# A tuned attention kernel of 1415 operations, reordered by a second search: new order and engine tables, refitted durations

## The chip, the cores and the metric

One core of one Trainium2 chip. The metric is the device time of one execution in microseconds (us). A time is the median of several executions. The profile is that of one of them, and its span (first to last instruction) is about 1.7 us shorter than the time of the same execution.

## The reference, cut to what matters

Two attention blocks run on the same 2048 x 640 input with 32 heads of 20, and a sigmoid gate mixes them. Block A is linear attention with a softmax feature map: projections, exponentials of both signs, normalisation, a key-value matrix per head, then a query side. Block B walks over four segments of 512 tokens: causal softmax attention inside each, plus a memory of the earlier ones.

```python
for s in range(N):                                   # block B, N = 4 segments of 512 tokens
    logits = jnp.einsum('bhqd,bhkd->bhqk', qs, ks) * scale + mask
    a_dot = jnp.einsum('bhqk,bhkd->bhqd', _softmax(logits, axis=-1), vs)
    num = jnp.einsum('bhld,bhde->bhle', pq, M)        # M, z: memory of the segments before
    den = jnp.einsum('bhld,bhd->bhl', pq, z)[..., None] + 1e-06
    outs.append(g * num / den + (1.0 - g) * a_dot)
    M = M + jnp.einsum('bhld,bhle->bhde', phi(ks), vs)
...
kv = jnp.einsum('bhsf,bhsd->bhfd', phi_k, v)         # block A, over all tokens
num = jnp.einsum('bhqf,bhfd->bhqd', phi_q, kv)
...
return g * a + (1 - g) * b
```

## The kernel before

The program is a list of 1415 operations. Each has the engines on which it may run, a duration that the author gave it, and the tiles that it reads and writes. A planner in the program, run when the kernel is built, plays the five instruction streams forward in time. At each step it takes, among the operations that can start within 0.12 us of the earliest one, that of the lowest priority number `pr`. What it decides is the order on each engine, the side of the 113 copies out of PSUM that may go to ACT or DVE, and the place of each tile in PSUM and SBUF. No duration reaches the chip; the order, the side and the places do.

```python
o.engs, o.dur, o.fn, o.pr, ... = engs, dur, fn, pr + NUDGE.get(len(self.ops), 0.0), name, dma, lat
...
while done < n:                                      # the planner, cut
    for e in STREAMS:
        ...
        if len(o.engs) > 1:
            b = {o.engs[0]: BIAS.get(o.idx, 0.0)}    # the engine table: ACT looks b us faster
            f = s + o.dur[e] - b.get(e, 0.0)
            if any(max(free[x], s) + o.dur[x] - b.get(x, 0.0) < f - 1e-6 for x in o.engs if x != e):
                continue
        ...
        lim = max(free[e], mn) + DELTA               # DELTA = 0.12 us
        ch = min(((o.pr, o.idx, s, o) for s, o in cands if s <= lim))
```

The operations that the argument touches, with PE = TensorE, DVE = VectorE, ACT = ScalarE, POOL = GpSimd:

```python
# block B: scores (QK, PE) -> exp (ACT) -> causal mask of the diagonal blocks (POOL, 128 of them) -> PV (PE)
mask(0, lambda: ex[:, :, 0:128], [[0, 4], [1, 128]], 512, [(0, 0), (0, 1)])
# -> combine (DVE): cmb, cmbp read PSUM, cmba adds two SBUF tiles into oB
# block B memory: keys transposed by DMA, then phi on DVE and ACT, SBUF alone
self.dma("sp", lambda c=c: pk[:, :, 128 * c:128 * (c + 1)], qk[:, c, 1, :], ..., transpose=True, dur=(1.3 if n else 1.7), lat=3.0, name="kT")
self.op("dve", 0.52, lambda e, tl=tl, tm=tm: e.tensor_tensor(pk[:, tl, :], pk[:, tl, :], tm[:, :], ALU.min), ..., name="pkmin")
# block A key side (DVE): sum, reciprocal, normalise, running sum "acc" of two SBUF tiles
# the small weight w_phi: its load is issued from POOL once the last key weights ("last") have landed
self.dma("pool", self.wphi[:, :, :], ..., pr=-39, lat=6.0, name="wphi", after=[last])
```

The softmax here doesn't subtract the row's maximum and nothing guards it: scores larger than these inputs give would overflow.

Of the kernel before, what the change touches and what calls it, by code (L numbers as in the profile page):

```python
# [7 lines left out]
ALU = mybir.AluOpType  # L8
AX = mybir.AxisListType

NUDGE = {6: 1.6, 7: 1.65, 8: -2.2, 9: -0.45, 11: -1.7, 19: -3.95, 22: 3, 23: 1.8, 24: -1.5, 35: -11.8, 36: -2.7, 37: 5.05, 40: 11.15, 62: 0.7, 63:
         2.15, 64: -1.4, 65: -7.8, 66: 0.95, 67: 6.15, 68: 17.2, 69: 9.2, 70: 3.6, 71: 13.15, 72: 4.2, 75: -8.85, 77: 1.3, 93: 4.7, 94: 16.3, 95:
         -0.65, 97: -1.6, 99: -7.9, 101: -10.25, 103: -15.25, 105: 1.1, 106: 9.7, 107: -3.35, 108: -1.55, 109: -0.15, 111: -1.75, 112: 3.45, 113:
         -2.1, 114: -8.75, 119: -5.35, 121: 2.9, 122: 3.2, 124: -0.8, 125: -0.7, 127: 6.1, 129: 3.1, 131: 5.9, 133: -6.55, 135: 5.9, 143: -3.6, 146:
         -1.7, 155: 7.9, 162: -9.4, 163: -4.5, 164: -3.3, 166: -12, 170: -3.35, 174: 1.85, 179: -5.05, 180: 6, 181: -6.5, 183: -6.3, 187: -3.45, 188:
         -4.45, 190: -8.2, 192: -2.65, 193: -11, 194: -6.6, 196: -10.35, 197: -2.45, 200: -0.65, 202: -10.9, 204: -3.1, 205: -2.9, 206: -7.45, 207:
         -4.25, 208: -8.5, 209: -3.3, 210: -14.45, 211: -7.8, 213: 4.2, 217: 0.75, 218: -3.2, 219: -10.25, 221: 4.05, 222: -12.25, 223: 42.5, 224:
         -9.75, 226: -1.55, 230: 0.7, 231: 6.1, 234: -5.6, 235: -1.3, 236: 5.7, 237: -6.8, 239: -1.75, 241: 6, 243: -0.95, 247: 2.05, 248: 4.6, 249:
         -4.9, 250: -13.95, 251: 1.2, 252: -9.8, 253: 3.7, 254: 5.35, 256: -5.533, 260: -5.8, 261: -2.8, 266: 1.75, 267: 3.85, 268: 3.05, 269: 1.071,
         270: 0.85, 271: -5.1, 273: -4.55, 277: 3, 282: 9.4, 283: 6.85, 284: -9.6, 285: 0.95, 286: -8.15, 287: 2.65, 288: 11.9, 289: -5.25, 290:  # L20
         -0.15, 291: 6.15, 292: 2.352, 293: -1.4, 294: 7.3, 295: 4.35, 296: -1.7, 297: 8.55, 298: -9, 299: -2.3, 300: -5.05, 301: -2.05, 302: 1.6,
         303: 1.5, 304: 1.85, 306: -1.25, 307: -4.35, 309: -3.65, 310: 7.4, 311: -1.45, 313: -1.7, 315: 1.4, 319: -2.75, 321: 0.85, 322: 3.45, 323:
         0.25, 324: -9.9, 325: 4.027, 328: 0.85, 332: 2.7, 333: 5.65, 335: 0.85, 336: 0.5, 337: -2.8, 338: -0.8, 339: 0.85, 341: 1.55, 344: -3.85,
         345: 6, 348: 3.1, 350: 1.35, 352: -1.1, 358: 4.35, 359: 8.25, 360: 4.05, 363: 2.35, 366: 0.75, 367: 2.55, 368: 8.3, 369: 0.4, 373: 3.9, 377:
         -5.8, 383: -0.75, 384: -0.55, 385: -2.35, 386: -0.4, 387: 2.85, 388: -2.35, 389: 3.95, 390: -14.3, 392: 2.6, 397: -7.05, 400: 1.55, 401:
         13.3, 402: 2.35, 403: -2.85, 404: 3.75, 405: -2.9, 407: -5.45, 411: 2.05, 412: 1.75, 413: 3, 415: -0.8, 416: 2.45, 417: -7, 418: -2.65, 419:
         -3.75, 420: -57.2, 421: 13.65, 422: 1.2, 426: 1.55, 430: 3.95, 434: 1.95, 435: 6, 437: -2.15, 438: -1.75, 439: -10.85, 441: -0.8, 445: -0.95,
         446: -2.6, 449: 0.35, 453: 3.75, 455: 10.95, 456: -1.45, 457: -4.15, 458: 7.35, 466: -13.2, 467: -0.9, 468: -2.9, 469: 0.4, 470: 6.4, 471:
         -1.942, 473: -5.4, 475: -1.75, 479: -0.35, 483: -2.15, 484: 0.45, 485: -12, 486: -19.7, 487: -8.75, 488: -8.05, 490: -3.1, 491: -13.85, 492:
         -10.1, 494: 2.6, 498: 3.258, 499: -1.2, 509: 4.15, 510: -5.5, 511: 9.8, 512: -3.25, 513: -2.6, 514: 8.8, 515: 0.55, 516: 12, 517: 7.6, 518:  # L30
         1.2, 519: -15.923, 521: 0.6, 522: 1.5, 523: -5.35, 524: -0.4, 525: 6.35, 530: -0.035, 531: 6.5, 532: 4.4, 533: -3.8, 534: 0.25, 535: -6.4,
         536: 4.9, 537: 3.15, 538: 2.672, 539: 14.3, 540: -2, 541: 3.35, 542: 2.85, 543: 6.7, 544: 0.007, 545: -3.65, 546: 0.5, 547: -9.45, 548:
         -1.95, 558: 1.65, 559: 4.45, 561: 4.1, 563: -4.15, 564: 0.1, 565: -1.95, 567: -0.25, 570: 1.8, 571: 0.2, 573: 3.5, 574: 21.8, 576: 4.25, 577:
         2.6, 578: 1.5, 579: -9.5, 581: 3.15, 582: 3.3, 583: 4.4, 584: 10.8, 586: 13.25, 587: 5.9, 590: 0.65, 591: 2.4, 592: -5.486, 594: 10, 596:
         -5.5, 597: -0.6, 600: 5.4, 604: -2.4, 605: -0.75, 608: 25.7, 610: -6.8, 611: -6.05, 612: -10.2, 616: -8.4, 619: 5.1, 620: 6.2, 626: -3.8,
         627: 3.05, 630: -28.25, 631: -13.3, 634: 4.85, 635: -8.65, 636: 5.15, 638: 2.55, 639: 0.85, 647: 11.35, 649: 1.85, 653: -2.35, 654: -1.35,
         658: 3.6, 659: 3.5, 660: -2.072, 662: -15.35, 664: -3.3, 668: -1.45, 672: 7.55, 673: 10.05, 678: 4.9, 679: -2.05, 683: -2.2, 687: -4.05, 688:
         2.05, 690: 10.05, 693: 4.75, 694: -3.2, 696: -3.55, 698: -3.55, 702: -2.45, 704: -2.45, 706: -1.65, 707: -6, 710: -8.75, 712: 14.75, 713:
         -2.8, 714: 10.25, 715: 3.15, 717: -3.7, 721: 1.45, 722: -5.1, 725: -8.9, 726: 0.25, 727: 6.4, 728: 5.1, 733: 0.35, 734: 2.7, 735: 18.4, 736:
         8.7, 737: 6.55, 738: 25.05, 739: 0.8, 740: 11.5, 741: 8.3, 742: 2.2, 743: 7.75, 744: 3.7, 745: -4.95, 746: 5.7, 747: -3, 748: 2.8, 753: 2.45,  # L40
         755: -0.35, 757: 5.35, 759: 0.574, 760: -6.65, 761: 0.3, 763: -0.233, 764: 2.35, 765: 6.2, 767: 3.5, 768: 5.5, 769: 5.75, 770: 2.8, 771:
         -1.45, 781: 2.2, 784: 0.45, 787: 16.15, 790: -7.7, 791: -0.85, 794: 1.6, 800: 14.35, 801: 7.1, 802: 4.15, 803: 21, 804: 12.15, 805: 6.2, 806:
         2.45, 807: 5.2, 809: 18.6, 810: 4.05, 811: 9.2, 812: 8.95, 813: 19.25, 814: 4.35, 816: 6.15, 817: 9.1, 819: -1.1, 823: -1.6, 827: -1.3, 828:
         -1.9, 834: -2.7, 835: -5.85, 838: -1.6, 842: 9.2, 843: -0.45, 845: 54.95, 849: 0.7, 850: -5.8, 853: -1.4, 857: -5.4, 860: 15.5, 861: 3.05,
         862: 2.2, 865: 6.6, 867: 26.85, 868: -6, 869: 3.15, 872: -12.3, 876: 3.95, 877: 11.35, 881: 10.1, 882: 3.85, 883: -1.35, 884: -3.55, 885:
         6.9, 887: 3.35, 891: -1.95, 895: -3.45, 896: -11.95, 900: 6.05, 902: -2.5, 903: 12.15, 904: -5.35, 906: -3.85, 910: -10.45, 911: -2.4, 917:
         0.05, 919: 7, 921: -13.35, 925: -12.75, 929: 7.15, 930: 6.35, 936: 1.45, 938: 1.25, 946: 4.95, 951: -2.5, 952: -9.6, 953: -7.2, 955: 4.85,
         959: -3.7, 961: -3.5, 962: -0.95, 963: 2.15, 967: -1.85, 968: 14.1, 969: 6.35, 970: -4.6, 971: 0.5, 972: -3.95, 973: 0.95, 975: -2.55, 976:
         14.9, 977: -5.4, 979: 9.25, 981: 0.1, 982: -4.7, 983: -4.75, 984: 0.85, 985: -7.75, 988: 4.1, 990: -1.75, 991: 1.45, 992: 0.45, 995: 1.8,
         997: 5.85, 999: 0.65, 1001: 9.85, 1003: -0.65, 1004: 4.7, 1005: 5.1, 1006: -6.1, 1007: 4.2, 1008: 0.85, 1009: 0.4, 1010: 5.15, 1011: 2.85,  # L50
         1012: 1.35, 1013: 1, 1014: -1.3, 1015: -1.15, 1016: 7.5, 1018: 10.8, 1019: 12.05, 1020: 0.25, 1021: -9.8, 1022: -3.95, 1023: 0.6, 1024: 5,
         1025: 5.85, 1026: -1.05, 1027: 3.6, 1029: -1.9, 1031: 0.3, 1034: 1.5, 1035: 1.45, 1036: -10.55, 1037: 3.55, 1038: 15.25, 1040: -0.65, 1041:
         5.25, 1042: -0.5, 1045: 0.1, 1047: -3.8, 1048: 8, 1051: 7.25, 1052: -4.4, 1053: -5.6, 1054: -3.05, 1055: 1.8, 1056: -0.4, 1058: -2.9, 1059:
         1.115, 1061: -0.15, 1062: 2.05, 1063: -1.7, 1064: -3.5, 1065: 5.3, 1066: -0.9, 1067: -7.6, 1068: 4.85, 1069: -2.2, 1070: -0.25, 1072: -6.9,
         1073: 1.9, 1075: -2.2, 1076: -5.7, 1077: -3.05, 1078: -3.05, 1079: 3.3, 1080: 2.464, 1081: 1.75, 1083: -1.1, 1084: 1.9, 1086: -1.1, 1087:
         -3.75, 1088: -8.6, 1090: 5.25, 1091: 2.85, 1092: 2.25, 1095: 1.95, 1097: -5.7, 1098: 1.95, 1101: 8.2, 1103: 0.4, 1104: 3.4, 1105: -7.75,
# [25 lines left out]
DH = 20  # L82
NT = 16
NCH = 5
# [90 lines left out]
class Graph:  # L175
# [6 lines left out]
    def op(self, engs, dur, fn, R=(), W=(), pr=0.0, claim=(), name="", dma=False, lat=0.0, after=()):  # L182
        o = Op()
        if isinstance(engs, str):
            engs = (engs,)
        if not isinstance(dur, dict):
            dur = {e: dur for e in engs}
# [356 lines left out]
class GatedMix(Graph):  # L544
# [399 lines left out]
    def b_mem(self, n):  # L944
# [5 lines left out]
        pk = self.sbt("pk", [128, 4, D], BF16, self.p_pk)  # L950
# [541 lines left out]
```

## Time and profile before

| | before |
|---|---|
| time, median of 4 (lowest, highest) | 321.23 us (321.08, 321.29) |
| span of the profile | 319.6 us |
| PE busy / idle | 297.3 / 22.3 us |
| DVE busy, 40 to 160 us | 115.6 of 120 us |
| granted clock | 1.0 throughout |

The lines for this are in the prediction. Two things to keep in mind: a matmul is drawn longer than it occupies PE, so idle time on PE is the better number; and lines are those of the program, so a helper's line stands for many operations.

### The profile page before, as it was taken

What the parts mean: (1) busy time and instruction counts of PE and PEld (TensorE: products, weight loads), DVE (VectorE), ACT (ScalarE), POOL (GpSimd) and SP (SyncE); (2) the same over time, 40 slices, a digit from 0 to 9 for tenths busy, and PEclk for the clock granted to TensorE, in tenths of its full rate; (3) what the DMA queues carried; (4) which work ended last, traced back from release to release, by engine and by line L of the source; (5) the groups of instructions that cost most, each with busy time, mean ns of one, the idle gap of its engine ahead of it and who ended that gap; (6) DMA issues with size and microseconds to landing.
All of it is one profiled execution on the core that took longest, in us unless ns stands there. A gap on an engine that the chain in (4) does not pass through costs nothing.

```text
span 319.6 us, 8900 instructions
## 1 busy us (share of the span) xinstructions
PE 297.3 (93%) x3822; PEld 174.5 (55%) x3822; DVE 245.9 (77%) x475; ACT 252.0 (79%) x302; POOL 110.5 (35%) x169
## 2 busy tenths in 40 slices
PE   8989899799899999879989999999999999988986
PEld 3444565366455565635565464756365565645664
DVE  5646898999999899999999996715775556857660
ACT  4377899988899889689988998769986869576612
POOL 6549223423243334235450234133222413223300
PEclk9999999999999999999999999999999999999999
DMA  7999884625314525972380102782044320521212
GB/s 246 294 217 195 101 145 80 138 43 92 76 21 84 106 43 83 112 132 49 116 175 1 24 2 22 128 128 55 23 43 64 84 62 11 55 60 27 64 23 82
DMA packets 70960, 28.01 MB, mean 88 GB/s; under 512 B 62410, under 2 KB 69002, under 8 KB 70922
## 3 DMA queue, kind: packets, MB, share of 16 engines
q1 hardware_dynamic: 70858, 27.41, 45.6%
q8 instruction: 30, 0.49, 0.7%
q0 software_dynamic: 64, 0.03, 0.1%
q14 instruction: 8, 0.07, 0.1%
HBM read 7.57 MB, written 4.59 MB: 38 GB/s over the span
## 4 chain that ended last, share of the span: by engine, by line
PE 54%; DVE 22%; ACT 15%; POOL 3%; DMA 2%; issue 2%; DVEq 0%; POOLq 0%
PE ps L1392 10%; PE ps L1104 8%; PE ps L896 6%; PE ps L1191 5%; PE ps L1293 5%; PE ps L1040 4%; ACT exb L1064 3%; ACT exb L1053 3%; DVE z L1206 3%; DVE E L1209 3%; ACT ET L1298 2%; DMA wphi<-in_A_w_phi_dram 2%; PE ps L1393 2%; ACT exb L1073 2%; PE ps L1354 2%; ACT E L1198 2%
## 5 line engine op out<-in xcount | busy, mean ns | idle before, releaser
L1058 POOL TENSOR_SCALAR_AFFINE_SELECT exb<-exb 128x512 bf16<-128x512 bf16 x96 | 69.9, 730 | 151.7 <-ACT exb L1053 81.4
L1053 ACT ACTIVATE exb<-ps 128x1024 bf16<-128x1024 f32 x64 | 62.1, 1024 | 11.1 <-PE ps L1040 11.0
L1064 ACT ACTIVATE exb<-ps 128x2048 bf16<-128x2048 f32 x32 | 60.0, 1876 | 7.7 <-PE ps L1040 7.6
L1104 PE MATMUL ps<-v1B,exb 128*128 128x42 bf16 (+1 forms) x1280 | 41.7, 181 | 3.0 <-DVE cb L1150 1.0
L1104 PEld LDWEIGHTS ps<-v1B,exb 128*128 128x128 bf16 x1280 | 38.8, 96 | 9.5 <-POOL exb L1058 2.8
L896 PE MATMUL ps<-xT,WB 128*128 128x512 bf16 x175 | 42.1, 380 | 1.4 <-DVE oB L1145 0.9
L1040 PE MATMUL ps<-qk 20*128 20x128 bf16 (+3 forms) x512 | 31.7, 301 | 4.2 <-ACT exb L1073 1.7
L1077 POOL TENSOR_SCALAR_AFFINE_SELECT exb<-exb 128x512 bf16<-128x512 bf16 x32 | 22.9, 736 | 30.5 <-ACT exb L1073 30.5
L1073 ACT ACTIVATE exb<-ps 128x2048 bf16<-128x2048 f32 x16 | 30.0, 1876 | 2.4 <-PE ps L1040 2.4
L896 PEld LDWEIGHTS ps<-xT,WB 128*128 128x128 bf16 x175 | 15.4, 98 | 21.0 <-issue 2.2
L1191 PE MATMUL ps<-WkA,xT 128*128 128x512 bf16 x80 | 23.5, 380 | 2.8 <-ACT exb L1053 1.1
L1198 ACT ACTIVATE E<-ps 128x640 bf16<-128x640 f32 x32 | 22.6, 705 | 4.3 <-PE ps L1192 3.8
L1209 DVE TENSOR_TENSOR E<-E,z 128x1280 bf16<-128x1280 bf16 x16 | 24.9, 1556 | 0.2
L917 PE MATMUL ps<-WvB,xT 128*128 128x512 bf16 x80 | 23.8, 380 | 1.1 <-DVE oA L1361 0.6
L1206 DVE TENSOR_REDUCE z<-E 128x64 f32<-128x1280 bf16 x16 | 23.6, 1474 | 1.6 <-ACT E L1198 1.5
L1298 ACT ACTIVATE ET<-ps 128x512 bf16<-128x512 f32 x40 | 22.9, 600 | 2.3 <-PE ps L1293 1.8
L1293 PE MATMUL ps<-xT,WqA 128*128 128x512 bf16 x100 | 24.1, 380 | 0.4 <-DVE ET L1337 0.4
L1191 PE MATMUL ps<-WvA,xT 128*128 128x512 bf16 x80 | 23.4, 380 | 0.5 <-ACT E L1198 0.4
L1392 PE MATMUL ps<-Wo,oTA 128*128 128x512 bf16 x75 | 22.0, 380 | 0.1
L1392 PE MATMUL ps<-Wo,oTB 128*128 128x512 bf16 x75 | 21.9, 379 | 0.0
L1040 PEld LDWEIGHTS ps<-qk 20*128 20x128 bf16 x512 | 8.9, 92 | 22.9 <-issue 6.7
L864 ACT ACTIVATE out<-ps 128x640 bf16<-128x640 f32 (+1 forms) x13 | 8.6, 663 | 14.9 <-PE ps L1393 13.3
(139 smaller groups left out, 598.7 us busy)
## 6 DMA issues: line engine op xcount, KB each, us to landing
out_dram<-out SPq DMA_DIRECT2D x15, 160.0 KB, 2.0
scr<-qk SPq DMA_DIRECT2D x16, 120.0 KB
qk<-scr SPq DMA_DIRECT2D x16, 120.0 KB
stq<-in_B_wq_dram SPq DMA_DIRECT2D x5, 160.0 KB, 4.2
WvB<-in_B_wv_dram SPq DMA_DIRECT2D x1, 800.0 KB, 5.3
WvA<-in_A_wqkv_dram SPq DMA_DIRECT2D x1, 800.0 KB, 7.8
Wo<-in_A_wo_dram SPq DMA_DIRECT2D x1, 800.0 KB
Wo<-in_B_wo_dram SPq DMA_DIRECT2D x1, 800.0 KB
```

The costliest lines, as they stand in the source:

```text
L896: r = e.matmul(self.pf(pt, 0, 0, LSEG), lhsT=self.WB[:, w, kc, 128 * c:128 * (c + 1)], rhs=xT[:, kc, LSEG * n:LSEG * (n + 1)], start=(kc = ...
L1040: r = e.matmul(self.pf(pts[i][0], pts[i][1], c0, N), lhsT=qk[32 * i:32 * i + DH, gg, 1, 128 * j:128 * (j + 1)], rhs=qk[32 * i:32 * i + DH, ...
L1053: self.op("act", d_act(1024), lambda e, p=p, pt=pt: e.activation(ex[:, 2 * p:2 * p + 2, off:off + 512], self.pbanks(pt, 0, 2, 512), ACT.Ex ...
L1058: self.op("pool", d_pool(n_el), lambda e: e.affine_select(view(), view(), pattern=pat, compare_op=ALU.is_ge, fill=0.0, base=0, channel_mul ...
L1064: return self.op("act", 1.79, lambda e: e.activation(ex[:, :, off:off + 512], four(pt), ACT.Exp, scale=scale), W=[(pt, i) for i in range(4 ...
L1073: self.lastmask = self.op("act", 1.79, lambda e: e.activation(self.exb[:, :, :, 1024:1280], four(p2).rearrange("p i (s c) -> p s i c", s=2 ...
L1104: r = e.matmul(self.pf(ad, b, 84 * q2 + 21 * i, w) if n else self.pf(ad, 0, 84 * qi + 21 * i, w), lhsT=ex[:, i, c0:c0 + 128], rhs=vt[:, j, ...
L1191: e.matmul(self.pf(pt, 0, 0, 512), lhsT=l, rhs=W[:, kc, 0:512], start=(kc == 0), stop=(kc == 4))
L1206: self.op("dve", 1.46, lambda e: e.tensor_reduce(rz[:, :], Ev(), axis=AX.X, op=ALU.add), R=[(E, 0), (E, 1)], W=[(rz, "*")], pr=pr, name="Z ...
L1209: self.op("dve", 1.46, lambda e: e.tensor_tensor(Ev(), Ev(), rz[:, :].rearrange("p (h o) -> p h o", o=1).to_broadcast([128, 2 * H, DH]), A ...
L1293: r = e.matmul(self.pf(pt, 0, 0, LSEG), lhsT=self.WqA[:, kc, 128 * c:128 * (c + 1)], rhs=xT[:, kc, LSEG * S:LSEG * (S + 1)], start=(kc == ...
L1392: e.matmul(self.pf(pt, 0, 0, 512), lhsT=l, rhs=self.Wo[:, c, 0:512], start=(c == 0), stop=(c == 9))
```

## The change

Its intent: run a second search over the order with durations fitted anew to the chip, and store what it found not as small corrections to hand-made priorities but as the intended start of every operation. The operations, shapes and tiles are the same.

```diff
-NUDGE = {6: 1.6, 7: 1.65, 8: -2.2, 9: -0.45, 11: -1.7, ...        # 749 corrections; cut
-BIAS = {120: -3.05, 121: -4, 122: -2.5, 124: -0.1, ...            # 25 entries; cut
+ORDER = (0.2, 0.39, 0.47, 0, 0.92, 2.19, 2.66, 1.53, 4.07, ...    # 1415 intended starts; cut
+         ... 312.81, 313.3, 309.89, 311.45, 311.95, 0, 0.29)
+BIAS = {63: -1, 65: 1, 67: -1, 69: 1, 71: -1, 96: 1, ...          # 113 entries: the sign is the engine; cut
-        ... o.pr, ... = ..., pr + NUDGE.get(len(self.ops), 0.0), ...
+        ... o.pr, ... = ..., ORDER[len(self.ops)], ...
-    key transposes of the memory: lat=3.0
+    key transposes of the memory: lat=3.8
-    PV: cnt * 0.026 + 0.07 * b + ...
+    PV: cnt * 0.026 + (0.07 if n == 0 else 0.02) * b + ...
-    pqmin 0.54, cmb 0.22 and 0.32, pqA 1.14, Uc 0.42
+    pqmin 0.47, cmb 0.20 and 0.29, pqA 1.09, Uc 0.38
```

## The prediction

> **What bounds the kernel now.** I read the page first (busy shares, slices, chain), then busy time per stage, then the waits of PE, then single groups of DVE instructions.
>
> ```profile
> PE 297.3 (93%) x3822; PEld 174.5 (55%) x3822; DVE 245.9 (77%) x475; ACT 252.0 (79%) x302; POOL 110.5 (35%) x169
> PE   8989899799899999879989999999999999988986
> DVE  5646898999999899999999996715775556857660
> ```
>
> PE is busy 297.3 of 319.6 us, at the full clock throughout, so only 22.3 us of PE idle time can be won by reordering: 7% if all of it went. The DVE row is full from about 40 to 190 us and half empty afterwards. The next view, busy time of each engine per stage (columns: stage, length, then PE, PEld, DVE, ACT, POOL busy with counts, granted clock, DMA share, GB/s), puts numbers to it.
>
> ```profile
> 40.00:80.00 40.00, 38.05 (x500) 22.85 (x497) 38.33 (x65) 36.23 (x45) 12.65 (x16) 1.00 0.55 99
> 80.00:120.00 40.00, 38.08 (x498) 22.04 (x497) 38.03 (x69) 36.59 (x43) 14.03 (x17) 1.00 0.34 66
> 120.00:160.00 40.00, 35.28 (x494) 20.93 (x492) 39.25 (x63) 35.66 (x41) 17.00 (x20) 1.00 0.62 100
> 160.00:200.00 40.00, 38.56 (x500) 22.06 (x493) 35.48 (x78) 36.37 (x48) 13.43 (x20) 1.00 0.24 44
> 200.00:240.00 40.00, 38.90 (x582) 23.50 (x579) 23.87 (x54) 32.95 (x41) 11.00 (x18) 1.00 0.47 75
> 240.00:280.00 40.00, 38.20 (x556) 23.23 (x549) 25.17 (x57) 29.34 (x32) 11.38 (x18) 1.00 0.33 55
> 280.00:320.00 40.00, 33.80 (x466) 21.94 (x466) 20.51 (x42) 19.39 (x18) 8.20 (x13) 1.00 0.19 51
> ```
>
> From 40 to 160 us DVE works 115.6 of 120 us: there DVE sets the pace, and PE loses 4.7 us in 120 to 160 alone. From 160 to 280 us PE is 96% busy and nothing else is full: PE sets the pace. In the last 40 us PE loses 6.2 us to waits along the last head group and to the drain. No single wait is worth much; the longest totals of PE in the waits view are these.
>
> ```profile
> PE ps L1040 <- ACT exb L1073: 1.7, 3, 0.8
> PE ps L1239 <- DVE cb L1150: 1.3, 2, 1.1
> PE ps L835 <- DVE zf L734: 1.3, 1, 1.3
> PE ps L1191 <- ACT exb L1053: 1.1, 1, 1.1
> ```
>
> So this is a well packed kernel with its loss spread over dozens of gaps of at most 1.3 us.
>
> **What the Trainium skill says.** "Perfetto Trace Analysis", section Identifying the Most-Contended Engine, warns that matmul busy time is no good measure of the headroom. The trace agrees: a 512 wide matmul is drawn with 380 ns (L896), while groups of five start 1.08 us apart, 217 ns each. I therefore count PE by start-to-start times below. "GPSIMD Engine Reference", section Specifications, says that GpSimd's SBUF interfaces are shared with VectorE, with contention for DVE instructions of two SBUF inputs or a two-port mode. The trace agrees: this group, which reads SBUF alone, has one size and a spread of a factor of two (durations min/median/max in ns).
>
> ```profile
> L962 DVE TENSOR_TENSOR pk<-pk,tmp x12: 426/485/916, 56.8 to 189.2; 128x640 bf16<-128x640 bf16 x12
> ```
>
> Sorting its twelve by whether a GpSimd mask runs beside them gives a mean of 759 ns with and 472 ns without; the cb group (L1150), which reads PSUM, gives 824 and 824. The longest exceed their group's lower quartile by 8.8 us in all between 40 and 160 us, where DVE is the bound. "Perfetto Trace Analysis", section Optimization Strategy, proposes interleaving regimes with different bounds; that is what a new order can do here, and the DVE row shows that it is not exhausted.
>
> **The change, part by part.** (1) Operations: the same 1415, so PE, ACT and POOL work stays and there is no gain in busy time. (2) Engine table: of 113 evacuations that may go to ACT or DVE, 20 change side, 10 each way. At about 0.6 us (ACT) or 0.68 us (DVE, L865 on 512 columns) each, the sums cancel: 0 us, apart from where they fall. (3) Durations: these are numbers in the program's own planner and cost nothing themselves. They say what the old plan misjudged. The PV matmuls of segments 1 to 3 lose 0.05 us per second half, 24 x 0.05 = 1.2 us, and the query projections 20 x (1.14 - 1.09) = 1.0 us; the trace has 0.79 and 1.09 us start to start, so the new numbers are right. That corrects 2.2 us of PE time that the old plan thought it spent and the chip never did. It is not a gain. The key transposes get 3.8 instead of 3.0 us of landing; the trace has a median of 3.4, up to 4.2. (4) Order: all that can gain. In the order of the new table 250 of the 348 PE operations keep their old sequence, 349 of 475 on DVE; it is reshuffled nearly everywhere after the first 45 us.
>
> The table gives an intended start for each operation, which I use as a statement of aim, setting it against starts in the trace:
>
> - first PV group, second half: aimed at 41.58, ran at 43.23 (difference 1.65)
> - second half of the last PV of segment 1: 159.83 against 165.10 (5.3)
> - the same of segment 2: 234.71 against 238.80 (4.1)
> - the same of segment 3: 298.13 against 304.40 (6.3)
> - last half output block on PE: 311.25 against 315.51 (4.3)
>
> Up to 43 us the order is nearly the old one, so the 1.65 us is not gain but slip: the trace's first matmul starts at 1.26 us where the table has 0.29, and the loads do the rest. What the table aims to win by order is thus 4.26 - 1.65 = 2.6 us. A second way: PE start-to-start times per kind (30th percentile of each) sum to 286.4 us; before lost 29.2 us beyond that between its first and last PE start, the table's starts imply 25.9. That is 3.3 us less, of which 0.97 us is the unreal early start left in the aim, so 2.3 to 3.3 us. By stage the aim is 13.3 instead of 17.1 us of loss up to 160 us, and 12.7 instead of 12.1 us after it: **all of the gain is in the DVE-bound part**, none in the PE-bound part.
>
> There the aim has DVE operations start between 80 and 120 us whose durations in the planner sum to 40.8 us, while the planner gives each instruction a fixed duration. The 8.8 us of stretching beside the masks is only partly in those. I expect the new order to miss its aim there by up to 1.5 us more, and to keep 2 to 3 us of the rest, since the refit removes one misjudgement (key transposes) and keeps others (0.10 to 0.15 us for small DVE instructions that take 0.17 to 0.25 us). On the tail, the last group still ends in a transpose, an evacuation and two half blocks. Sum: 0 (busy) + 0 (engines) - 3.0 (order, between 2 and 4) + 0 (tail) = -3.0 us, so 321.2 - 3.0 = 318.2 us, 0.9% faster.
>
> **Rivals.** *The aim is met in full.* The table's last store starts at 313.3; before's last evacuation ends at 317.5 and its time is 321.2, so with the same 3.7 us behind it the time would be 317.0. If in addition the early slip were cured, 315.4. For: the planner was nearly right last time within a few tenths of a us per stage. Against: the early slip comes from parts that are hardly touched. *The DVE stretch eats the gain.* A dense new order puts more SBUF-only DVE work beside masks; three more us of it in a stage where DVE has 4 us spare would leave 320 to 322 us. For: 25 stretched instructions there now, averaging 0.35 us, and no rule in the planner against them. Against: the number of masks is the same, and before suffered already. *A new wait on PE*: an evacuation moved to the other engine holds PSUM banks and PE waits a few tenths of a us more at each of 20 places: 320 us. For: ACT is at 36 of 40 us in the same stage, so a misplaced evacuation queues. Against: 10 each way, chosen with the order.
>
> **Range and chances.** The centre is 318.2; full success gives 315.4 to 317, failure 320 to 321. Eight in ten: 315.7 to 320.4. Over 2% faster means below 314.9: that needs more than the table itself asks for, 5%. Over 2% slower means above 327.6, which would take a new wait of a kind that the list above doesn't have, 1%. Within 2%: 94%.
>
> **What will show it.** Right: PE busy stays at 297 to 298 us (same instruction counts), its idle time falls from 22.3 to about 19 us, and the fall lies in the stages up to 160 us (PE busy in 120 to 160 above 36.5 us). DVE stays at 38 us or more per 40 from 40 to 160. The second half of the first PV starts at about 43.2 us again, that of the last PV of segment 1 between 161 and 163. Wrong: if the stages up to 160 us are unchanged and the time is won after 200 us, then PE's tail and not DVE was what the order improved; if the L962 and acc (L1218) groups grow in mean duration while PE idles longer, the stretch ate it; if the first 43 us shorten, I misread the early slip.

## The result, and the profile after

| | before | after |
|---|---|---|
| time, median of 4 (lowest, highest) | 321.23 us (321.08, 321.29) | 316.22 us (316.04, 317.37) |
| span of the profile | 319.6 us | 314.4 us |
| PE busy / idle | 297.3 / 22.3 us | 297.8 / 16.6 us |

The ratio is 0.9852 with a 95% interval of 0.9829 to 0.9876. A ratio here is the mean time of one kernel's fast runs over that of the other's of the same rounds, so not quite the ratio of the medians. The gain is 5.0 us where 3.0 was predicted.

The page after, with the rows of busy time and of slices for PE and DVE:

```profile
PE 297.8 (95%) x3822; PEld 175.0 (56%) x3822; DVE 244.8 (78%) x476; ACT 251.4 (80%) x301; POOL 107.3 (34%) x169
...
PE   8999999999999989889999999999999999888996
...
DVE  4667798999999999999999895726677477857660
```

The work is the same and PE's share rose. Busy time of each engine per stage after (columns as in the prediction; the last stage ends at 314.4):

```profile
40.00:80.00 40.00, 39.28 (x527) 24.03 (x526) 37.94 (x66) 37.74 (x48) 12.27 (x16) 1.00 0.69 106
80.00:120.00 40.00, 38.58 (x477) 21.53 (x476) 38.96 (x70) 37.14 (x44) 13.76 (x18) 1.00 0.32 60
120.00:160.00 40.00, 35.34 (x536) 21.98 (x534) 39.22 (x66) 36.16 (x41) 18.46 (x22) 1.00 0.66 120
160.00:200.00 40.00, 39.52 (x539) 23.20 (x537) 34.07 (x80) 35.48 (x46) 10.34 (x16) 1.00 0.22 33
200.00:240.00 40.00, 39.59 (x527) 23.29 (x525) 24.68 (x57) 31.84 (x38) 12.12 (x19) 1.00 0.30 64
```

PE gained 1.2 us of busy time from 40 to 80 us, nothing from 120 to 160 us, where it still loses 4.7 us to a full DVE, and 1.0 and 0.7 us in the next two stages. Windows of fixed time mix what was moved with what was won, so I also set the two kernels side by side at equal PE work. Each PE operation counts with the start-to-start time of its kind (the sum is 286.4 us); the table shows when each kernel reached a given amount.

| PE work done, us | before at | after at | after ahead by |
|---|---|---|---|
| 10 | 11.6 | 12.2 | -0.7 |
| 30 | 34.7 | 33.5 | 1.2 |
| 50 | 54.9 | 53.7 | 1.2 |
| 60 | 67.2 | 64.3 | 2.8 |
| 90 | 99.8 | 96.0 | 3.9 |
| 130 | 146.9 | 142.6 | 4.3 |
| 210 | 232.3 | 227.8 | 4.5 |
| 230 | 253.8 | 248.4 | 5.4 |
| 286 (end) | 316.8 | 311.5 | 5.2 |

Four fifths of the gain are made in the first 147 us, in steps of 1.2 us up to 35 us, 1.6 us around 60 us and 1.1 us up to 100 us; the rest is one step of 0.9 us around 240 us.

The first step has names. These are the waits of PE between 2 and 40 us, first before, then after (columns: who waited for whom, total us, times, longest us).

```profile
PE ps L1191 <- DVE WkA L865: 1.1, 1, 1.1
PE ps L851 <- DVE BD L811: 0.7, 1, 0.7
PE ps L917 <- ACT WkA L864: 0.3, 1, 0.3
```

```profile
PE ps L1211 <- DVE WkA L885: 0.3, 1, 0.3
PE ps L871 <- ACT eg L941: 0.2, 1, 0.2
```

(The lines of the program have moved down by 20.) Before, PE waited 0.7 us for the block matrix BD, made of the late weight w_phi, and 1.1 us for a copy of WkA that stood behind four small coefficient operations on DVE. After, the two are nearly gone. The landing of w_phi has a part in this: it came 7.9 us after its issue in the trace before and 6.4 us in the one after. Where it took 8.1 us (e3, which begins like the new kernel) and 7.8 us (e8, which has its tables), PE waited 2.0 and 2.1 us for BD, so this step is not won in every execution.

The rival that I had given most weight, DVE instructions stretched beside POOL's masks, did not move. Summing what exceeds each group's lower quartile as in the prediction gives 8.8 us before and 8.7 us after between 40 and 160 us. Of the two groups that I had named as a sign, pk fell from 640 to 583 ns on the mean and acc grew from 562 to 591, while PE idled less. The pk group, after:

```profile
L982 DVE TENSOR_TENSOR pk<-pk,tmp x12: 477/488/916, 55.0 to 178.1; 128x640 bf16<-128x640 bf16 x12
```

### The profile page after: what moved, and what is told of

The parts are those of the page before. It is cut to its first block, busy times and chain, and to the rows that moved or that the text cites. A ratio compares the mean times of both kernels' runs of the same rounds, so it can differ in the third digit from the quotient of the medians.

```text
span 314.4 us, 8893 instructions
## 1 busy us (share of the span) xinstructions
PE 297.8 (95%) x3822; PEld 175.0 (56%) x3822; DVE 244.8 (78%) x476; ACT 251.4 (80%) x301; POOL 107.3 (34%) x169
## 4 chain that ended last, share of the span: by engine, by line
PE 59%; DVE 25%; ACT 12%; issue 1%; POOL 1%
PE ps L1412 10%; PE ps L1313 7%; PE ps L916 7%; PE ps L1124 7%; PE ps L1060 4%; ACT exb L1084 4%; DVE E L1229 3%; PE ps L937 3%; PE ps L1211 3%; DVE z L1226 3%; PE ps L1413 2%; DVE cb L1170 2%; DVE acc L1238 2%; ACT exb L1093 2%; PE ps L1374 2%; ACT exb L1073 2%
## 5 line engine op out<-in xcount | busy, mean ns | idle before, releaser
L1078 POOL TENSOR_SCALAR_AFFINE_SELECT exb<-exb 128x512 bf16<-128x512 bf16 x96 | 68.3, 713 | 153.0 <-ACT exb L1073 84.0
L916 PE MATMUL ps<-xT,WB 128*128 128x512 bf16 x175 | 43.0, 380 | 0.7 <-DVE oB L1165 0.4
L1060 PE MATMUL ps<-qk 20*128 20x128 bf16 (+3 forms) x512 | 31.7, 301 | 2.8 <-ACT exb L1084 1.1
L1097 POOL TENSOR_SCALAR_AFFINE_SELECT exb<-exb 128x512 bf16<-128x512 bf16 x32 | 21.8, 703 | 27.9 <-ACT exb L1093 27.9
L1060 PEld LDWEIGHTS ps<-qk 20*128 20x128 bf16 x512 | 8.9, 92 | 20.8 <-issue 6.8
L1170 DVE TENSOR_TENSOR cb<-ps,cs 128x640 bf16<-128x640 f32 x24 | 19.8, 823 | 0.7
```

The costliest lines, as they stand in the source:

```text
L916: r = e.matmul(self.pf(pt, 0, 0, LSEG), lhsT=self.WB[:, w, kc, 128 * c:128 * (c + 1)], rhs=xT[:, kc, LSEG * n:LSEG * (n + 1)], start=(kc = ...
L1060: r = e.matmul(self.pf(pts[i][0], pts[i][1], c0, N), lhsT=qk[32 * i:32 * i + DH, gg, 1, 128 * j:128 * (j + 1)], rhs=qk[32 * i:32 * i + DH, ...
L1078: self.op("pool", d_pool(n_el), lambda e: e.affine_select(view(), view(), pattern=pat, compare_op=ALU.is_ge, fill=0.0, base=0, channel_mul ...
```

## The experiments

Twelve kernels ran. Nine of them differ from the two kernels only in tables or planned numbers, so any difference is order, side or place. The others also free one load from a wait (e10, e11) or shorten the masks (e12). Most needed an order that the planner's rule cannot express exactly, for example the new order up to some time and the old one after it. For those the rule was replaced by fixed lists of one engine each; the planner then only lays out the tiles and the waits. Replaying the new kernel's own lists this way gives its plan exactly.

```diff
# "fixed lists", used in every experiment below that names them
-                ch = min(((o.pr, o.idx, s, o) for s, o in cands if s <= lim))
+                if at[e] == len(SEQ[e]): continue
+                o = self.ops[SEQ[e][at[e]]]
+                s = est(o, e) if o.nleft == 0 else None
+                if s is not None and (best is None or s < best[0]): best = (s, e, o)
...
+            at[best[1]] += 1
```

The table gathers the results; the planner's sum is the time that the program's own planner reckons with the durations that stand in that kernel. Unless said, a kernel has the new durations (e10 has the old ones). Medians of the kernel before on the same chips were 321.4 to 321.8 us. The new kernel itself ran in its own round only, so differences from it are between medians of different chips; I lean on them where a trace shows the same.

| run | order | sides | planner's sum | chip, median (lowest, highest) | ratio to before, 95% interval |
|---|---|---|---|---|---|
| before (old durations) | old | old | 320.47 | 321.23 (321.08, 321.29) | 1 |
| after | new | new | 315.56 | 316.22 (316.04, 317.37) | 0.9852 (0.9829, 0.9876) |
| e1 | new | old | 322.96 | 324.82 (324.32, 326.16) | 1.0113 (1.0082, 1.0143) |
| e2 | old | new | 322.15 | 324.02 (323.18, 324.84) | 1.0076 (1.0052, 1.0100) |
| e3 | new to 43 us, then old | likewise | 320.29 | 322.53 (321.62, 325.07) | 1.0043 (0.9994, 1.0092) |
| e4 | old to 43 us, then new | likewise | 317.78 | 318.57 (318.38, 318.98) | 0.9909 (0.9893, 0.9924) |
| e6 | old to 120 us, then new | likewise | 318.42 | 320.48 (319.63, 322.60) | 0.9965 (0.9905, 1.0024) |
| e7 | old tables, the planner chooses | | 359.19 | 370.64 (369.48, 371.29) | 1.1509 (1.1449, 1.1568) |
| e8 | new tables, old durations, the planner chooses | | 323.61 | 321.99 (321.70, 324.31) | 1.0017 (0.9959, 1.0076) |
| e9 | new, laid out with old durations | new | 318.80 | 317.88 (317.39, 320.10) | 0.9887 (0.9829, 0.9945) |
| e10 | old, w_phi loaded early | old | 320.47 | 323.54 (321.18, 324.04) | 1.0026 (0.9980, 1.0072) |
| e11 | new, w_phi loaded early | new | 315.56 | 317.79 (317.51, 318.38) | 0.9862 (0.9821, 0.9903) |
| e12 | new, masks cut short | new | 315.56 | 312.26 (312.22, 316.74) | 0.9734 (0.9658, 0.9809) |
| e13 | a third search | own | 318.25 | 322.00 (320.82, 322.92) | 1.0005 (0.9971, 1.0039) |

### e1 and e2: order without the sides, sides without the order

My prediction booked the engine table with 0 us. It and the expectations say that 20 copies change side, ten each way. That is one too many: the plans differ in 19, ten to DVE and nine to ACT, and the pages count 475 and 476 instructions on DVE. The edits: fixed lists; in e1 the 19 go back to their old engine, at the place in time that they have in the new order; in e2 the old order keeps its sequence and the same 19 go to the new engine.

> The new order on every engine, but the 20 evacuations that changed engine stand on their old one, at the place that their time gives them. Theory order: the sequence carries the gain and the sides cancel (10 each way), so 316 to 318 us. Rival engine table: the sides are what made the sequence fit, so the gain is lost, 321 us or more. The planner's own sum for it is 322.96 us.

> The old order on every engine, with the 20 evacuations on their new engine. Theory order: no gain, 321 to 322.5 us. Rival engine table: some gain by itself, 319 us or less. The planner's sum is 322.15 us.

Each half alone is slower than the kernel before: e1 by 1.1%, e2 by 0.8%. e1 is 8.6 us slower than the new kernel by the medians, with a granted clock of 0.995 in the profiled run. Set side by side with it at equal PE work, it loses 2.5 us up to 160 us of work and 4.2 us at once between 240 and 250. These are two of PE's longest waits in e1 between 250 and 300 us, then the longest of the new kernel between 245 and 295:

```profile
PE ps L1099 <- DVE ET L1396: 2.2, 2, 1.2
PE ps L1413 <- ACT exb L1112: 1.3, 1, 1.3
```

```profile
PE ps L1124 <- DVE cb L1170: 1.0, 1, 1.0
```

The score matmuls (L1099, in the new kernel L1060) wait for DVE's product ET (L1396). It always runs on DVE, so it is not one of the moved copies; the chain of e1 shows the moved copy behind it (start, duration, what).

```profile
260.30 1.88 ACT exb L1123
262.18 0.48 ACT rT L923
262.70 0.40 PE ps L1394
263.13 1.29 DVE ET L1396 x2
264.47 0.40 PE ps L1099 x8
```

The copy rT, on DVE in the new kernel, is back on ACT and stands behind an exponential of 1.88 us. PE waits 0.93 us for rT and 0.95 us for ET, and from 265.1 us on its clock is at half for 3.4 us. So the rival of my prediction, a new wait on PE at a moved evacuation, is real, but as the price of taking order and sides apart. Neither showed a share of the gain by itself: they were found together and carry the time together.

### e3 and e4: the first 43 us

The edits: fixed lists, spliced at 43 us of the plan. The question was whether the early 1.2 us is kept to the end.

> The new order for what starts before 43 us (in the plan), the old order for the rest. In the two traces the new order is 1.2 us ahead at that point. Theory kept: the early 1.2 us stays to the end, 320.0 us. Rival absorbed: the old rest waits for something else anyway, as my prediction took it (no gain in the first 43 us), 321.2 us.

> The reverse of the last: the old order before 43 us, the new one after. Theory kept: 1.2 us of the gain is lost, 317.4 us. Rival absorbed: 316.2 us. If far more is lost (319 or over), the rest of the new order only fits behind its own start.

e4 lost 2.35 us against the new kernel by the medians. The trace shows it 1.2 to 1.3 us behind until 150 us of work, as before was, and 0.9 us more at 160 to 170, where `PE ps L1099 <- DVE qk L924` appears with 0.8 us: a bank given to another tile than in the new kernel, the same wait as in e9 below (the plans of e4 and e9 both put that tile in a bank last read by this copy). That wait is 0.8 of the 1.2 us by which e4 missed what I expected. So the early 1.2 us is part of the gain and is not given back later.

e3 did not show its half. Its profiled run was its slowest, 325.07 us: the weight w_phi landed late, PE waited for the matrix made of it, and the granted clock fell in two slices.

```profile
PE ps L910 <- DVE BD L870: 2.0, 1, 2.0
```

In that trace the 2.0 us stay exactly 2.0 us behind before until 210 us of work, which says that an early shift is kept. But the two undisturbed executions took 321.62 where 320.0 was expected, and there is no trace of them. This stays open; e10 below shows one way in which such a lead is lost.

### e6: where along the kernel

The edit: fixed lists, old up to 120 us, then new.

> The old order for what starts before 120 us (in the plan), the new one after. At equal PE work the new kernel's trace is 3.0 to 3.9 us ahead by then and 5.2 us at the end. Theory kept by stages: 1.3 to 2.2 us of the gain remains, 319 to 320 us. Rival all before 160 us from the start on: nothing remains, 321 us. Rival tail: most remains, 317 us.

The three executions at full clock took 319.6 to 321.0: the gain falls to between 0.4 and 1.8 us when only the part after 120 us is new. That is what the table of progress says (4.3 us up to 147, 0.9 after). The fourth and slowest is the profiled one: a transposed key tile landed late, DVE stood 2.8 us and PE 2.2, and 3.4 us at half clock followed. I return to this with e10 and e13.

### e7, e8 and e9: what the refitted durations do

I had written that the durations cost nothing themselves. e7 is the kernel before with the new durations alone, e8 the new kernel with the old ones; in both the planner chooses by its rule. e9 keeps the new order by fixed lists, and only the planner's clock, by which it lays out tiles, has the old durations.

> The old priority and engine tables with the refitted durations: one half of the diff alone. Theory: durations have no cost of their own but choose what the planner takes next, so the old table, tuned for the old ones, makes another order, and a bad one: 340 to 360 us (the planner's sum is 359.2). Rival: durations only describe, the order hardly changes: 321 us.

> The new tables with the old durations: the other half alone. Theory: again another order, part of the gain lost, 320 to 324 us (the planner's sum is 323.6). Rival: the new table alone carries the gain: 316 us.

> Each engine keeps exactly the new order and side, but the planner lays out PSUM banks and buffers with the old durations. Theory: the durations matter through the order alone, so 316 to 317 us, although the planner's own sum is 318.8. Rival: the layout of banks that follows from the refit is part of the gain: 318 us or more.

e7 is 15% slower. A table tuned by a search is a key to one set of durations: the planner takes, of what can start within 0.12 us, the lowest number, so shifts of 0.05 us make it take others, and the old corrections then push in the wrong direction. e7's planner knew of 359 us; the chip took 11 us more. The row of granted clock and the last stage (columns as before) show where:

```profile
PEclk9999999999999999899998999999995888555589
...
300.00:370.00 70.00, 38.83 (x507) 25.18 (x507) 17.23 (x41) 26.19 (x23) 11.97 (x19) 0.68 0.08 21
```

PE is busy 38.8 of the last 70 us, and its clock is granted at 0.68 there: in this trace a PE that waits also computes slower afterwards.

e8 came out like the kernel before (ratio 1.0017): the new table without its durations carries nothing, although its intended starts are the same (w_phi landed late in its trace, so part of that may be chance). e9 lost 1.2 us to the new kernel in the trace, in two jumps, of which the larger, at 155 to 170 us of work, has one wait that the new kernel does not have there:

```profile
PE ps L1079 <- DVE qk L904: 0.8, 1, 0.8
```

The order on every engine is the same, so this is the PSUM bank: planned with other durations, a tile gets a bank whose last reader ends later on the chip. So the durations reach the chip by two ways, the order that they let the planner choose (e8 lost 5.8 us by the medians, its banks included) and the banks (1.2 us by the traces; 1.7 by the medians, but the intervals of the two ratios overlap).

### e10 and e11: the late weight alone

The first step of the gain was a shorter wait for w_phi and for a copy behind it. Could that be had directly? The edits: `after=[last]` is taken from the loads of w_phi and beta and they go first on POOL's queue, with the old order (e10) and the new (e11), both by fixed lists.

> The old order; only the load of the small weight w_phi (and of beta) no longer waits for the landing of the last key weights, and stands first on GpSimd. In the trace before it lands at 19.3 us and PE waits 0.7 us for the block matrix made of it. Theory: the early gain of the new kernel is this load coming 2 us earlier by chance (6.4 instead of 7.9 us to landing), so 320.5 us here, with the 0.7 us wait gone, and steadier from run to run. Rival: the wait is absorbed later, 321.2 us.

> The new order with the same edit. Its trace shows no wait for this load, so the median stays at 316.2 us. Theory: the run of 317.4 us among four was one in which it landed late, so no run over 317 us here. Rival: the load now takes bandwidth from the first weights and delays the start, 317 us or more.

No. e10 is not faster than before and no steadier. Yet its trace shows the early gain: BD no longer keeps PE waiting, and set against before weight load by weight load (the order on PE is the same) e10 is 1.3 us ahead at 40 us. By 56 us it is 2.7 us behind: as in e6, DVE stands for a transposed key tile.

```profile
DVE tmp L997 <- DMA pk<-qk: 3.0, 1, 3.0
PE ps L935 <- DVE qk L904: 2.2, 1, 2.2
```

The wait of 2.2 us and the 3.4 us at half clock after it, worth 1.7 us, are the 3.9 us lost. So the lead was real in this execution and did not last. e11 is steady (six executions at full clock within 0.9 us) but 1.6 us slower than the new kernel by the medians: the loads moved ahead are in the way of the first key weights, and PE waits for those.

```profile
ACT WB L862 <- DMA stk<-in_B_wk_dram: 1.6, 1, 1.6
PE ps L955 <- ACT WB L862: 1.4, 1, 1.4
```

In the new kernel the same wait of ACT is 0.9 us and none of PE follows. The load was where it belonged.

### e12: the stretch beside the masks

The rival that I gave most room did not move in the change, so its size was untested. Here the 128 masks clear 8 columns of one head instead of 512, at the same places and with the planned durations left as they were, so the plan is the same. The scores are wrong on purpose (the comparison's tolerance did not notice).

```diff
-mask(0, lambda: ex[:, :, 0:128], [[0, 4], [1, 128]], 512, [(0, 0), (0, 1)])
+mask(0, lambda: ex[:, 0:1, 0:8], [[0, 1], [1, 8]], 512, [(0, 0), (0, 1)])    # and likewise the others
```

> The new order, the 128 masks of GpSimd cut to 8 columns of one head: a wrong result on purpose, the same instructions, waits and plan. In the new trace some 26 DVE instructions between 40 and 160 us are stretched beside masks, 8.7 us in all. Theory of the prediction (the stretch eats part of the gain, DVE being the bound there): the stretch falls to 2 to 4 us and 2 to 5 us of time are won, 311 to 314 us. Rival (the order on every engine is fixed and its other waits take over): under 1 us, 315.3 to 316.2 us.

312.26 us, 4.0 less than the new kernel: three executions at 312.2 to 312.3, the fourth at 316.74 with its clock at 0.995. Three groups of the new kernel: the larger group of masks, the PSUM reading combine, and the SBUF-only running sum (busy us and mean ns of one after the bar):

```profile
L1078 POOL TENSOR_SCALAR_AFFINE_SELECT exb<-exb 128x512 bf16<-128x512 bf16 x96 | 68.3, 713 | 153.0 <-ACT exb L1073 84.0 <-ACT exb L1084 62.6 <-ACT eg L941 4.2
L1170 DVE TENSOR_TENSOR cb<-ps,cs 128x640 bf16<-128x640 f32 x24 | 19.8, 823 | 0.7
L1238 DVE TENSOR_TENSOR acc<-acc,TT 128x640 bf16<-128x640 bf16 x31 | 18.3, 591 | 0.3
```

and the same in e12:

```profile
L1117 POOL TENSOR_SCALAR_AFFINE_SELECT exb<-exb 128x8 bf16<-128x8 bf16 x96 | 26.6, 278 | 191.5 <-ACT exb L1112 105.4 <-ACT exb L1123 78.1 <-ACT eg L980 5.8
L1209 DVE TENSOR_TENSOR cb<-ps,cs 128x640 bf16<-128x640 f32 x24 | 19.8, 823 | 0.7
L1277 DVE TENSOR_TENSOR acc<-acc,TT 128x640 bf16<-128x640 bf16 x31 | 15.0, 483 | 0.4
```

The masks take 26.6 instead of 68.3 us. The running sum falls from 591 to 483 ns, the combine keeps its 823 ns to the nanosecond, and DVE's busy time falls from 244.8 to 231.6 us. By the measure of the prediction, the stretch from 40 to 160 us falls from 8.7 us to nothing. Masks that end sooner could also win time directly, since PV waits for them. Where the time is won speaks against that. PE's order is the same, so the two traces can be set side by side weight load by weight load.

| at, in the new kernel | 15 us | 40 us | 160 us | 280 us | end |
|---|---|---|---|---|---|
| e12 ahead by, us | 0.41 | 0.80 | 3.85 | 3.86 | 4.06 |

From 40 to 160 us, where DVE is full, 3.05 us are won. After 160 us, where 64 of the 128 masks stand, it is 0.2 us, though they are shortened as much. The first 0.4 us come before the first mask (27.5 us), so the masks have no part in them. So the stretch costs about 3 us, in the part where DVE sets the pace, and the change neither removed nor raised it.

### e13: a third search

If order is what carries time, a further search should win more. Mine started from the new kernel's lists and lowered a recomputed time instead of the planner's sum.

> A further search of my own over order and side, with the operations and durations of the new kernel. Its aim was not the planner's sum but a recomputation: the planner lays out the tiles, then the fixed order of each engine is played once more with every dependency, with durations fitted to the traces of the two kernels. By this measure the new kernel takes 313.7 us and the chip 2.5 to 3.0 more; the found order takes 312.6. Theory (order is the quantity that carries time, and this measure is exact to about half a microsecond): the chip is 1.1 us below the new kernel, so 315.1 (314.6 to 315.7), ratio to the kernel before 0.981. Rival (after two searches what a third one finds is the error of its model, and waits that the measure doesn't see come back): 316.2 or more, ratio 0.985 or above.

The rival holds, and by far: 322.0 us, 5.8 above the new kernel, with the granted clock at 0.989 or 0.995 in all six executions. At equal PE work e13 is 2.0 us behind from the start, wins 1.3 of that back by 130 us of work, then falls to 6.0 us behind between 130 and 140, and stays there to the end. Both losses have names. At the start the search had moved the clearing of a zero tile behind other small DVE operations, to 2.5 us instead of 0.9, and PE's first matmul needs it. The second is this stretch of DVE's timeline (start, duration, and idle time before it with its releaser):

```profile
141.49 0.54 DVE L1267 RECIPROCAL z<-z 128x64 f32<-128x64 f32 x1
145.62 0.49 DVE L1277 TENSOR_TENSOR acc<-acc,TT 128x640 bf16<-128x640 bf16 x1 [3.59 <-DMA TT<-E]
```

DVE stood 3.6 us for a transposed tile of block A. In the timeline of the SP queue its issue is

```profile
139.11 3.83 SPq L769 DMA_TRANSPOSE TT<-E  x1
```

3.83 us for an issue that takes 1.4 in the median of its kind. Four transposes and two stores had gone into the queue in the seven microseconds before it; that they are the reason is likely, but not shown. It landed 6.5 us after its issue. My measure, like the planner, gives every such transfer 1.36 us to issue and 3.6 more to land, whatever else is under way. The planner had the tile there at 140.4 us; DVE ran 1.4 us behind the plan by then, so 141.8 on the trace's clock, and the tile came at 145.6, 3.8 us late. Of these 1.5 us are the longer issue and landing. The other 2.2 or so are a late start: the plan has this issue at 135.5, and the queue was up to 5.0 us behind its plan by then. DVE takes its operations in order, so what stood behind waited too, and PE ran dry:

```profile
PE ps L1099 <- DVE cb L1209: 2.8, 1, 2.8
```

After the wait the granted clock halves (stages of 2 us; the third number from the end):

```profile
148.00:150.00 2.00, 0.85 (x5) 0.24 (x6) 1.90 (x6) 0.19 (x1) 0.00 (x0) 0.58 0.70 130
150.00:152.00 2.00, 2.00 (x9) 1.01 (x8) 1.97 (x5) 1.75 (x2) 0.00 (x0) 0.50 0.37 95
152.00:154.00 2.00, 2.00 (x10) 0.93 (x8) 1.70 (x4) 1.40 (x2) 0.00 (x0) 0.50 0.00 0
154.00:156.00 2.00, 2.00 (x17) 0.76 (x15) 1.92 (x2) 0.77 (x3) 0.00 (x0) 0.71 0.00 0
```

So one late landing cost the 5.3 us of the jump: 2.8 of waiting and some 2.5 of clock. The four stages agree: what is missing from full clock there is 2 x (0.42 + 0.50 + 0.50 + 0.29) = 3.4 us, of which PE still waited through the first part. The planner's own sum, 318.25, had been more careful than my measure and still 3.8 us too low. No version that beats the new kernel and computes the right result came out.

## Why the prediction was right or wrong

**The mechanism was right in the main.** Busy time gave nothing (PE 297.3 and 297.8 us), and the whole gain is idle time of PE. It came by order, though only together with sides and banks (e1, e8, e9). Four fifths of it lie in the first 147 us, about 3.1 of the 5.2 us in the part where DVE is full, and e12 shows that DVE sets the pace there. The time lay within the range, near its lower edge of 315.7; the gain lay outside the 2 to 4 us that the sum allowed for order. Neither the stretch nor a new wait on PE took anything back.

**The mis-sized term is "- 3.0 (order, between 2 and 4)"; it measured 5.0.** Two steps made it small.

- "Up to 43 us the order is nearly the old one, so the 1.65 us is not gain but slip." The first 35 us gave 1.2 us: the waits for BD (0.7 us) and WkA (1.1) all but went, e4 loses the 1.2 when that part is old, and the first PV group started at 42.01 us, not at "about 43.2 us again" (the prediction calls it the second half; its 41.58 and 43.23 too are the start of the first). I had written that this would mean I misread the early slip; so it does. A few places changed in an order that is otherwise the same, just ahead of PE's first long run, were the point, with an early landing of w_phi where it came.
- "I expect the new order to miss its aim there by up to 1.5 us more." The new order missed its plan by less than the old one had: around 172 us the trace of before is 3.3 us behind its own plan and that of the new kernel 0.9. I had booked the refit as a correction of PE time, "not a gain", and did not ask what it does to the old order. It does two things that nearly cancel: the shorter durations alone take the planner's sum of the old order from 320.47 to 319.58 us, the longer key transposes alone to 321.89, both to 321.00. The new order has 315.56. That is 5.4 us with both orders on one scale; with each on its own durations the sums differ by 4.9. Either was a better number to predict from: the chip gave 5.0. My own comparison set the new plan's aim against the old trace and then took a further miss off it.

**The term "+ 0 (engines)" nearly holds as a sum and misleads as a statement.** Copies swap sides 10 to 9, but without them the new order is 2.7% slower than with them (324.82 against 316.22 us), and with them alone the old order is 0.8% slower.

**"Durations cost nothing themselves" is incomplete.** They choose the order (e7, e8) and the PSUM banks (e9, 1.2 us by the traces).

**Signs in the profile.** PE idle 16.6 us (I said about 19); DVE 37.9, 39.0 and 39.2 us of 40 (I said 38 or more); last PV of segment 1 at 160.73 (I said 161 to 163). Wrong: PE's busy time from 120 to 160 us was to exceed 36.5 us and is 35.34, since the gain came before that stage; and 0.9 us came after 200 us, where I had expected none.

**The rivals.** "The aim is met in full" (317.0 us) is nearest; the chip went 0.8 us below it, which fits an early slip cured in part, as that rival had allowed. "The stretch eats the gain" did not happen, though e12 shows that the stretch is worth about 3 us. "A new wait on PE" did not happen in the change, and did in e1, e4 and e9.

**Open.** Why the undisturbed executions of e3 show none of the 1.2 us (a key tile that lands late, as in e10, is a guess); how much of the early gain hangs on the landing of w_phi; and what the 0.8 us are that e12 wins before 40 us.

## What to carry to other kernels

When a plan is searched with refitted durations, compare the planner's sums of the two orders before predicting (4.9 us here, each on its own durations, and 5.4 on one scale; the chip gave 5.0). The sum of a new plan set against the trace of the old one gave 2.3 to 3.3. Even the sums agree with the chip only roughly: it lay 0.7 to 0.8 us above them in these two kernels, but 1.6 below in e8, 3.8 above in e13 and 11.4 above in e7. Treat order, engine choice, buffer layout and the durations that they were searched with as one object; order, sides or durations alone were worth nothing or less than nothing. A search stops being useful where its model is blind, here at transfers that queue behind one another: give those slack in the order (not tried here), because one landing 3.8 us late cost 5.3 us.

## What the Trainium skill lacked or had wrong

- "GPSIMD Engine Reference", section Specifications, names the contention with VectorE but not what it costs a whole kernel. Here it is about 3 of 316.2 us (e12); a 128x640 sum of two SBUF tiles takes 591 ns on the mean with the masks and 483 ns without, one that reads PSUM 823 ns in both.
- "TensorE: Matmul & The Clock Gate", section HAM oscillation — how this bites in real kernels, gives as abstract rule that PE should have no idle gap above about 3.4 us. Here a single wait of 2.8 us, in a kernel whose PE is 94% busy, was followed by 6.8 us at half clock in e13, and single waits of 2.0 to 2.2 us by 3.4 us at half clock in e3, e6, e8 and e10. In the traces of before and after, whose longest gap is 1.1 us, the clock stays full. The same page's section What's actually happening gives half the full clock as the throttled state; the 0.50 in two stages of e13 agrees.
- No page among those I read says how far the landing of one DMA transpose on a queue depends on those ahead of it. Here the same transposes of a 128x1280 tile (TT, issue to landing) took 3.4 to 5.5 us in the new kernel, 4.2 as median, and 3.5 to 6.5 us in e13 between 113 and 148 us; the issue itself took 1.3 to 4.1 and 1.3 to 3.8 us.
